# First channel layer of the third batch's first 512 tokens by seven half-width products instead of eight

## The chip, the cores and the metric

One core of one Trainium2 chip. The metric is the device time of one execution in microseconds (us); the times of before are three such executions. TensorE is PE, its weight load PEld, VectorE is DVE, ScalarE is ACT, GpSimd is POOL, and SyncE, which issues every DMA here, is SP.

## The reference

Four batches, 8 heads, 768 tokens of 64 values per head, so 512 values per token. Per batch: attention over a local window and over block means, then a mixer along the tokens and one along the channels.

```python
x  = attention(q, k, v)                  # window |i-j| < 16, and means of blocks of 32
h  = relu(x.T @ w_tok1) @ w_tok2         # 768 -> 256 -> 768 along the tokens
u  = x + h.T
h2 = relu(u @ w_ch1) @ w_ch2             # 512 -> 1536 -> 512 along the channels
out = u + h2
```

All of it is float32.

## The kernel before, in words

**Precision.** A float32 operand is split into a high and a low part, and each product is made of three (high by high, high by low, low by high). So a 128-row weight block against a stretch of tokens costs three matmuls.

**Tiling.** Batches 0 to 2 run through the channel mixer in two parts of 512 and 256 tokens, each in 12 slots, one for a chunk f of 128 of the 1536 channels. In a slot `ch1` (L1018, matmuls at L1027, PSUM tile `hp`) makes the chunk: four weight blocks c=0..3 by three products, 12 matmuls of 512 or 256 columns. ACT writes relu(hp) as the high part of `h` (L1039), DVE the low part (L1044), and `ch2` (L1054, matmuls at L1070, tiles `acc`) adds the chunk's share to the four outputs, again 12 matmuls. `ch1` of a slot stands ahead of `ch2` of the slot before, so PE has work while `h` is split.

**Beside it.** The attention of batch b+1 runs in the slots of batch b: scores `sc` (L513), the scan on DVE that adds the mask and finds each row's lowest (L527, called the mask scan here), exponentials on ACT (L537), a transpose on DVE (L598), the way through DRAM (`away` L602, `eT` L620), and the product with the values `av` (L645). Heads go in pairs: `sc_24` and `sc_25` are the first half of a pair's scores, and pair 12 is the first of batch 3. Near the end of batch b stand `tok1_all` of batch b+1 (tiles `t1q`, L883) and its `tok2` (L942, tiles `up`, L966): DVE adds `up` to the transposed `x` (`xT`, L982), ACT and DVE split the sum into `u` (L990, L996). In batch 2 `tok2` of the 256 tokens stood in slots 2 to 5.

**The last batch** already goes by seven products for eight, with weights that are mixed beforehand: `mixes` (L1127) builds on POOL and ACT four combinations of the weight blocks of a pair of chunks (i, i+6), and SP parks them in DRAM (`mix_w1h`, `mix_w1l` for the first channel layer, L1198). The table `MIXES` says in which slot of which batch each is built.

**What sets the order.** Every piece of work is an entry with an engine, a modelled duration, what it reads and writes, and a rank. A planner (L162) runs through them in modelled time; on each engine the ready entry of the lowest rank goes next. The result is a fixed queue per engine, and an instruction that waits holds all behind it on its engine. SP's queue is one too, and each DMA also waits for the eighth DMA before it.

```python
R_H, R_EVAC, R_ATT, R_LATER, R_W = range(5)
BANKS = {"start": ["att", "att", "acc0", "acc1"], 0: ["att"], 1: ["att", "att", "acc2", "acc3"]}
```

PSUM has two banks for `hp` ("mm"), two for the attention ("att"), and one for each of acc0 to acc3.

Of the kernel before, what the change touches and what calls it, by code (L numbers as in the profile page):

```python
# [10 lines left out]
F32 = mybir.dt.float32  # L11
# [234 lines left out]
def tile_attention_mixer(  # L246
# [72 lines left out]
    state = {"phase": "start", "gate": []}  # L319
# [472 lines left out]
    def tok1(b, p):  # L792
        x2, a = x_t[b, p]
        pt = bank(f"t1p_{b}_{p}", ["mm", "mm", "acc3"])

        def products():
# [16 lines left out]
    def tok1x(b, g):  # L813

        x2 = x2_t[b, g]
# [49 lines left out]
    def tok1_all(b):  # L865

        pts = [att_bank(f"t1q_{b}_{k}") for k in range(DTOK // P)]
        xk = [key for p in range(NP) for key in x_keys(b, p)]
# [71 lines left out]
    T2_KEYS = [(w, (i, k)) for w in (wt2h, wt2l) for i in range(3) for k in range(2)]  # L940

    def tok2(b, half, p):  # L942
        if b == B - 1:
            return tok2_last(half, p)
        (x2, a), t1 = x_t[b, p], t1_t[b, p]
        h0, nt = H0[b][half], HT[b][half]
        pt = bank(
            f"up_{b}_{half}_{p}",
            ["mm", "mm", "acc3"] if state["phase"] == "start" else BANKS[state["phase"]],
# [6 lines left out]
        def products():  # L956
# [17 lines left out]
            reads=([] if far else x_keys(b, p)) + t1_keys(b, p) + T2_KEYS,  # L974
# [41 lines left out]
    h_t = {}  # L1016
# [37 lines left out]
    def ch2(b, half, f):  # L1054
        h, nt = h_t.pop(f), HT[b][half]
        n = 512 // nt
        if f == 0:
# [5 lines left out]
        last = f == NF - 1  # L1063
        slots = [sums[o][0] for o in range(0, NC4, n)]

        def products(os):
            for o in os:
                slot, c0 = sums[o]
                for w, part in (("w2h", 0), ("w2l", 0), ("w2h", 1)):
# [3 lines left out]
                        start=(f == 0 and w == "w2h" and part == 0 and o % n == 0),  # L1073
# [3 lines left out]
        reads = [(h, 0), (h, 1)] + weight_keys(("w2h", "w2l"), f)  # L1077
# [127 lines left out]
    def mixed(name, i, sets, view, keys, behind=()):  # L1205
# [8 lines left out]
            reads=[(src, 0), (src, 1)], writes=keys, kb=131 * (hi - lo), behind=behind,  # L1214
        )

    def mixed_weight(name, i, sets, f, halves, behind=()):
# [3 lines left out]
            weight_keys((name,), f, halves), behind,  # L1221
# [29 lines left out]
    def tok2_last(half, p):  # L1251
        b, t1, u = B - 1, t1_t[B - 1, p], sums_at(half, p)
        pt = bank(f"up_{b}_{half}_{p}", EIGHT if half else BANKS[1])

        def products():
# [10 lines left out]
            "pe", 1.08, products, reads=t1_keys(b, p) + T2_KEYS, writes=[(pt, 0)], rank=R_ATT  # L1266
# [42 lines left out]
    def out_of(pt, to, other, func=AF.Copy):  # L1309
# [15 lines left out]
        )  # L1325

# [616 lines left out]
```

## Time and profile before

| what | value |
|---|---|
| three executions | 558.75, 559.75, 560.01 us; median 559.75 |
| the profiled execution | 557.6 us, its span 555.8 us (1.8 us lie around the span) |
| granted TensorE clock | 1.000 over the span: the 2.4 GHz level |
| PE busy | 543.1 us, 98% of the span |
| DVE, ACT, POOL busy | 330.6, 251.8, 246.7 us (59%, 45%, 44%) |
| DMA | 101.10 MB, mean 182 GB/s |

The page is read as follows: PE is busy nearly all the time, so a change shows in the time either through the time that PE's own instructions take, or through a wait that it brings into PE's queue. The profiled execution is 2.15 us below the median of the three.

### The profile page before, as it was taken

To read this page: it belongs to the slowest core of one execution; us is meant where nothing else is said; L and a number is where in the kernel's file an instruction comes from. 1 tells how busy PE (TensorE), PEld (TensorE's weight loads), DVE (VectorE), ACT (ScalarE), POOL (GpSimd) and SP (SyncE) were. 2 spreads that over 40 slices of the span, in tenths; PEclk is the share of its full clock that TensorE was granted. 3 is DMA by queue.
4 is the path that set the end of the run, shared out by engine and by line. 5 is a ranking of instruction groups with operands and counts; after the bars stand their busy time and mean duration, and the time that the engine had idled before them with its cause. 6 is when DMAs were issued, how large, how long until landed. Compare 5 with 4: busy or idle time off the path is not lost.

```text
span 555.8 us, 12577 instructions
## 1 busy us (share of the span) xinstructions
PE 543.1 (98%) x4549; PEld 478.7 (86%) x4549; DVE 330.6 (59%) x922; ACT 251.8 (45%) x784; POOL 246.7 (44%) x362
## 2 busy tenths in 40 slices
PE   7799999999999999999999999999999999999997
PEld 4589788889989878888799987878889999999997
DVE  5897799988463355553553257344352066569992
ACT  5895666526485443322414325243433443356410
POOL 0356688726383933310058404467869853000000
PEclk9999999999999999999999999999999999999999
DMA  8992568745658147867676216787696543932732
GB/s 294 343 255 85 184 197 261 245 131 190 228 163 256 38 153 208 224 190 210 160 229 157 96 30 202 164 235 199 168 276 147 135 166 116 317 102 86 238 113 86
DMA packets 125743, 101.10 MB, mean 182 GB/s; under 512 B 70000, under 2 KB 105456, under 8 KB 125680
## 3 DMA queue, kind: packets, MB, share of 16 engines
q1 hardware_dynamic: 125680, 100.29, 60.8%
q8 instruction: 36, 0.59, 0.5%
q14 instruction: 27, 0.22, 0.1%
HBM read 70.18 MB, written 28.31 MB: 177 GB/s over the span
## 4 chain that ended last, share of the span: by engine, by line
PE 88%; DVE 5%; POOL 3%; ACT 2%; issue 1%; POOLq 0%; DVEq 0%; ACTq 0%
PE acc L1070 28%; PE hp L1027 27%; PE sc L513 4%; PE av L645 4%; PE t1q L883 3%; PE up L966 3%; PE x L1297 2%; PE y L1297 2%; PE z L1297 2%; PE pz L1297 2%; PE up L1259 2%; PE pw L1297 1%; PE pv L1297 1%; PE px L1297 1%; PE pr L1297 1%; PE w L1297 1%
## 5 line engine op out<-in xcount | busy, mean ns | idle before, releaser
L1070 PE MATMUL acc<-h,w2h 128*128 128x256 f32 (+1 forms) x576 | 153.9, 339 | 0.0
L1027 PE MATMUL hp<-u,w1h 128*128 128x256 f32 (+1 forms) x576 | 143.9, 339 | 0.3 <-DVE u L1010 0.3
L1070 PEld LDWEIGHTS acc<-h,w2h 128*128 128x128 f32 x576 | 100.5, 188 | 13.9 <-ACT h L1039 1.7
L1027 PEld LDWEIGHTS hp<-u,w1h 128*128 128x128 f32 x576 | 98.0, 189 | 12.9 <-issue 1.1
L1027 PE MATMUL hp<-u,w1l 128*128 128x256 f32 (+1 forms) x288 | 96.9, 336 | 0.0
L1070 PE MATMUL acc<-h,w2l 128*128 128x256 f32 (+1 forms) x288 | 96.4, 335 | 0.0
L537 ACT ACTIVATE e<-e,den 128x120 f32<-128x120 f32 x192 | 73.5, 385 | 48.8 <-DVE den L527 37.9
L1044 DVE SCALAR_TENSOR_TENSOR h<-hp,h 128x512 fp32r<-128x512 f32 (+1 forms) x72 | 39.8, 552 | 83.9 <-ACT h L1039 83.8
L1039 ACT ACTIVATE h<-hp 128x512 fp32r<-128x512 f32 (+1 forms) x72 | 35.1, 487 | 104.2 <-PE hp L1027 104.0
L1027 PEld LDWEIGHTS hp<-u,w1l 128*128 128x128 f32 x288 | 54.4, 189 | 5.8
L1070 PEld LDWEIGHTS acc<-h,w2l 128*128 128x128 f32 x288 | 54.2, 188 | 5.2
L527 DVE CUSTOM_DVE_ANT_0 e<-sc,mask_sb 128x120 f32<-128x120 f32 x192 | 41.8, 277 | 14.9 <-PE sc L513 14.3
L537 ACT ACTIVATION_READ_ACCUMULATOR e<-e,den 128x1 f32 x192 | 36.3, 189 | 0.0
L651 POOL TENSOR_SCALAR rec<-den 128x6 f32<-128x6 f32 x32 | 8.5, 266 | 58.7 <-ACT e L537 57.0
L1110 POOL TENSOR_TENSOR ot<-ot,u 128x512 f32<-128x512 f32 (+1 forms) x24 | 24.4, 1045 | 21.4 <-DVE ot L1102 19.9
L469 DVE TENSOR_REDUCE vs<-vb 96x8 f32<-96x256 f32 (+1 forms) x40 | 18.0, 461 | 21.0 <-DMA vb<-in_vb 20.7
L513 PE MATMUL sc<-k,q 64*64 64x120 f32 x768 | 27.7, 271 | 2.2 <-DVE k L390 1.2
L513 PEld LDWEIGHTS sc<-k,q 64*64 64x64 f32 x768 | 20.3, 132 | 10.8 <-issue 7.9
L645 PEld LDWEIGHTS av<-v,eT 120*64 120x64 f32 x768 | 24.1, 138 | 5.3 <-issue 3.5
L966 PE MATMUL up<-wt2h,t 128*128 128x512 f32 (+1 forms) x96 | 28.4, 353 | 0.1
L645 PE MATMUL av<-v,eT 120*64 120x64 f32 x768 | 26.7, 224 | 1.3 <-DVE den L527 0.8
L381 DVE TENSOR_REDUCE ks<-k 128x24 f32<-128x768 f32 x16 | 15.1, 946 | 19.9 <-DMA k<-in_kw 19.8
(248 smaller groups left out, 1042.5 us busy)
## 6 DMA issues: line engine op xcount, KB each, us to landing
w<-in_w_ch SPq DMA_DIRECT2D x48, 256.0 KB
k<-in_kw SPq DMA_DIRECT2D x16, 720.0 KB
v<-in_vw SPq DMA_DIRECT2D x32, 288.0 KB
q<-in_q SPq DMA_DIRECT2D x16, 384.0 KB
away<-e SPq DMA_DIRECT2D x16, 384.0 KB
eT<-away SPq DMA_DIRECT2D x64, 96.0 KB
w<-in_w_tok SPq DMA_DIRECT2D x12, 256.0 KB
vb<-in_vb SPq DMA_DIRECT2D x32, 96.0 KB
```

The costliest lines, as they stand in the source:

```text
L469: lambda: nc.vector.tensor_reduce(out=s.t[:VB, rows], in_=slot.t[:VB], axis=AX, op=ALU.add),
L513: nc.tensor.matmul(tiles[j].t[c * QT : (c + 1) * QT, i * NC : (i + 1) * NC], lhsT=qt.t[rows, t * QT : (t + 1) * QT], rhs=kt.t[rows, t, :], ...
L527: nc.vector.tensor_tensor_reduce(out=e.t[:, j, i * P : i * P + NC], in0=tiles[j].t[:, i * NC : (i + 1) * NC], in1=mask_sb[:, mv, :], op0=A ...
L537: nc.scalar.activation(ei, ei, AF.Exp, bias=den_t[n].t[:, 1, T : T + 1], scale=-1.0, accum_out=den_t[n].t[:, 0, T : T + 1],)
L645: nc.tensor.matmul(pv[cs, T], lhsT=eT[:NC, T % (TT // 2), cs], rhs=v.t[:NC, 2 * T + c], start=True, stop=True,)
L966: nc.tensor.matmul(pt.t[:, :nt], lhsT=t1.t[:, part, ks], rhs=w.t[:, k, h0 : h0 + nt], start=(far and k == 0 and i == 0), stop=(k == DTOK / ...
L1027: nc.tensor.matmul(pt.t[:, :nt], lhsT=block(w, f, c), rhs=us[c].t[:, part], start=(i == 0), stop=(i == len(ops) - 1),)
L1039: lambda: nc.scalar.activation(h.t[:, 0], pt.t[:, :nt], AF.Relu),
L1044: lambda: nc.vector.scalar_tensor_tensor(out=h.t[:, 1], in0=pt.t[:, :nt], scalar=0.0, in1=h.t[:, 0].bitcast(F32), op0=ALU.max, op1=ALU.sub ...
L1070: nc.tensor.matmul(slot.t[:, c0 : c0 + nt], lhsT=block(w, f, o), rhs=h.t[:, part], start=(f == 0 and w == "w2h" and part == 0 and o % n == 0),
L1110: lambda view=view, u=u: nc.gpsimd.tensor_tensor(out=view(), in0=view(), in1=u.t[:, 1].bitcast(F32), op=ALU.add),
L1297: nc.tensor.matmul(pt.t[:, :cols], lhsT=w[wp][0](), rhs=z.t[:, zp], start=first and seen == 0, stop=final and seen == 3 * len(ops) - 1, sk ...
```

## The change

In batch 2 the first channel layer of the first 512 tokens is made in another way for four of the six pairs of chunks, (0,6), (1,7), (2,8) and (5,11). Let the four 128-row blocks of `u` be two halves of the sum and the 512 tokens two halves of 256. A pair is then a 2x2 by 2x2 block product, 8 products of 256 columns, or in the matmuls of before 2 x 12 of 512 columns. It becomes 7 products of 6 matmuls of 256 columns: 42 for 24. The order of the 12 chunks becomes 10, 9, 4, 3, which are made as before, then the pairs.

- **Token side** (`differences`, once, at slot 0 of batch 2): four combinations "1" to "4" of the blocks of `u`, each split again: 8 x (three DVE operations of 128x256 at L1439, an ACT copy at L1447, a low part at L1453 on DVE or POOL). They lie where the token weights lay (tags `wt1`, `wt2h`, `wt2l`), which are therefore parked in DRAM in batch 0 (`keep_token`) and brought back in slots 16 and 18 of batch 2 (`return_token`).
- **Weight side**: the mixed weights of the last batch, 32 loads of 128 KB (`load_set`, L1221) into five half chunks of the plain weights, which are parked and brought back also (`keep_block`, `return_block`, ten DMAs each). The mixes of the second layer move from slots 5 to 9 of batch 2 to batches 0 and 1, others to slots 6 to 12.
- **Per pair**: `first_of` (4 products in the two "mm" banks `s7b`, `s7a`, then one ACT copy and three DVE additions), `second_of` (3 products, two DVE sums, four ACT relus and four DVE low parts of 256 columns, where two and two of 512 stood).
- **Moved for it**: `tok2` of the 256 tokens of batch 2 goes from slots 2 to 5 to slot 0, with `x` in the tag `wt1` (`x_home`) and the banks acc2 and acc3; the attention of batch 3 is spread over another stretch of slots (`A01`).

```diff
-    MIXES = {(0, 12): [('w1', 0, 'h')], ... (2, 5): [('w2', 0, 't1', 0), ('w2', 0, 't1', 1)], ...}
+    MIXES = {
+        ...
+        (0, 8): [("w2", 0, "t1", 0)], (0, 9): [("w2", 0, "t1", 1)],
+        ...
+    }
+    A01 = -4, 25
+    KEEP, BACK = (0, 18, 20, 22), (16, 18, 18)
+    ENDS = [f for f in range(NF) if f % HF not in SEVEN]
+    SEQ = [(0, f) for f in reversed(ENDS)] + [(0, f) for i in SEVEN for f in (i, i + HF)]
...
-            u1s = (2, 3, 4, 5)
+            u1s = (2, 3, 4, 5) if b < SB else (0, 0, 0, 0)
...
+            if b == SB and slot in NEXT:
+                job, i = NEXT[slot]
+                at = job(i)
...
+            if b == SB and slot == 0:
+                differences()
...
+    def differences():
+        ...
+        for to, x, y in (("1", "12", "11"), ("2", "22", "1"), ("3", "22", "12"), ("4", "21", "2")):
+            for c in range(2):
+                ...
+                for (a, i), (d, k), op in (
+                    ((xv, 0), (yv, 0), ALU.subtract), ((None, 0), (xv, 1), ALU.add),
+                    ((None, 0), (yv, 1), ALU.subtract),
+                ):
+                    add("dve", 0.37, ...)
+                add("act", 0.36, ...)
+                eng = "dve" if to in "12" else "pool"
+                add(eng, 0.37 if eng == "dve" else 0.7, ...)
...
+    def first_of(i):
+        B2, A = mm_bank(f"s7b_{i}"), mm_bank(f"s7a_{i}")
+        ...
+            (B2, "w", 0, (ring[i, 0], 0), "2", True, []),
+            (B2, "y", QS, (ring[i, 1], 0), "1", False, [(B2, "w")]),
+            (A, "p", 0, (i, 0), "11", True, []),
+            (A, "x", QS, (ring[i, 2], 0), "3", False, [(A, "p")]),
...
+    def second_of(i):
+            (B2, "y", QS, (ring[i, 3], 0), "22"),
+            (A, "p", 0, (i, 1), "21"),
+            (A, "x", QS, (i + HF, 1), "4"),
```

The planner makes a new order of every engine from this. Three places of it follow. In the names, `up_2_0_3` is batch 2, first part, block 3; `e_12_0` is pair 12, first half.

DVE at the start of batch 2 before the change, from the last `u` on; the first scan of pair 12 stands right behind the splits:

```order
L982 TENSOR_TENSOR xT_2_0_2_4102<-up_2_0_2_4277,xT_2_0_2_4102 128x512
L996 TENSOR_TENSOR u_2_0_1_4296<-xT_2_0_1_4071,u_2_0_1_4296 128x512
L996 TENSOR_TENSOR u_2_0_2_4302<-xT_2_0_2_4102,u_2_0_2_4302 128x512
L982 TENSOR_TENSOR xT_2_0_3_4286<-up_2_0_3_4289,xT_2_0_3_4286 128x512
L996 TENSOR_TENSOR u_2_0_3_4335<-xT_2_0_3_4286,u_2_0_3_4335 128x512
L1044 SCALAR_TENSOR_TENSOR h_1_1_11_4349<-hp_1_1_11_4321,h_1_1_11_4349 128x256
L527 ISA e_12_0_4316,den_24_4391<-sc_24_0_4371,mask_sb_71 128x120
```

The same place of the change. Between `u_2_0_2` and the first mask scan stand the four `x_home` additions and the last output of batch 1 (`ot`):

```order
L1007 TENSOR_TENSOR u_2_0_2_4538<-xT_2_0_2_4358,u_2_0_2_4538 128x512
L993 TENSOR_TENSOR x_home_4370<-up_2_1_0_4530,x_home_4370 128x256
L993 TENSOR_TENSOR x_home_4370<-up_2_1_1_4541,x_home_4370 128x256
L1112 TENSOR_TENSOR ot_1_1_0_4482<-acc_1_1_2_3933,u_1_1_2_3287 128x256
L1112 TENSOR_TENSOR ot_1_1_0_4482<-acc_1_1_2_3933,u_1_1_3_3368 128x256
L993 TENSOR_TENSOR xT_2_0_3_4521<-up_2_0_3_4512,xT_2_0_3_4521 128x512
L993 TENSOR_TENSOR x_home_4370<-up_2_1_2_4561,x_home_4370 128x256
L993 TENSOR_TENSOR x_home_4370<-up_2_1_3_4579,x_home_4370 128x256
L1007 TENSOR_TENSOR u_2_0_3_4603<-xT_2_0_3_4521,u_2_0_3_4603 128x512
L527 ISA e_12_0_4527,den_24_4614<-sc_24_0_4589,mask_sb_71 128x120
```

And between the scans of the two halves of pair 12 in the change stand five operations of the differences, one low part, the transpose and the split of `h`:

```order
L1453 TENSOR_TENSOR diff_wt2h_4607<-diff_tmp_4519,diff_wt2h_4607 128x256
L1439 TENSOR_TENSOR diff_tmp_4519<-diff_tmp_4519,u_2_0_1_4510 128x256 x2
L1439 TENSOR_TENSOR diff_more_4650<-u_2_0_2_4538,diff_wt2h_4607 128x256
L1439 TENSOR_TENSOR diff_more_4650<-diff_more_4650,u_2_0_2_4538 128x256
L1439 TENSOR_TENSOR diff_more_4650<-diff_more_4650,diff_wt2h_4607 128x256
L598 STREAM_TRANSPOSE e_12_0_4527<-e_12_0_4527 128x768
L1055 SCALAR_TENSOR_TENSOR h_2_0_10_4673<-hp_2_0_10_4616,h_2_0_10_4673 128x512
L527 ISA e_12_1_4570,den_24_4614<-sc_24_1_4655,mask_sb_71 128x120
```

So the scans of pair 12 stand behind more work on DVE, and the scores of pair 13 (`sc_26`, `sc_27`) use the banks that they free.

SP before the change, around the four DMAs that bring back pair 13's second half (`eT_13_1`):

```order
L602 DMA away_13_1_4818<-e_13_1_4704 128x768
L1198 DMA mix_w1h_4_4700<-wa_w1_4_1_4737 512x1x128
L1198 DMA mix_w1l_4_4708<-wc_w1_4_1_4814 512x1x128
L620 DMA eT_13_1_4885<-away_13_1_4818 32x24x32 x4
L602 DMA away_14_0_4929<-e_14_0_4887 128x768
```

And in the change. The five loads ahead of it overwrite weight sets which PE must have read; the last of them waits for the second product of `s7b_2`:

```order
L1221 DMA w1h_2_1332<-mix_w1h_5_4210 128x256
L1221 DMA w1l_2_1339<-mix_w1l_5_4250 128x256
L1221 DMA w1h_3_1496<-mix_w1h_5_4210 128x256
L1221 DMA w1l_3_1519<-mix_w1l_5_4250 128x256
L1221 DMA w1h_3_1496<-mix_w1h_5_4210 128x256
L620 DMA eT_13_1_5229<-away_13_1_5125 32x24x32 x4
L1221 DMA w1l_3_1519<-mix_w1l_5_4250 128x256
```

`eT_13_1` now stands behind set loads that are released by PE.

## Rows read from the trace of the kernel before

**Rows 1.** The page: busy time of the engines, and the chain of work that ended last, by engine.

```profile
PE 543.1 (98%) x4549; PEld 478.7 (86%) x4549; DVE 330.6 (59%) x922; ACT 251.8 (45%) x784; POOL 246.7 (44%) x362
PE 88%; DVE 5%; POOL 3%; ACT 2%; issue 1%; POOLq 0%; DVEq 0%; ACTq 0%
```

**Rows 2.** Windows of 25 us: busy time of PE, PEld, DVE, ACT and POOL, the granted clock, the DMA share and GB/s. Batch 2's first part runs from 328.87 to about 409 us.

```profile
225.00:250.00 25.00, 25.00 (x199) 20.23 (x198) 13.61 (x45) 8.66 (x32) 5.39 (x12) 1.00 0.79 217
...
325.00:350.00 25.00, 25.00 (x194) 20.79 (x193) 14.24 (x55) 10.26 (x42) 5.74 (x11) 1.00 0.48 132
350.00:375.00 25.00, 25.00 (x199) 20.38 (x198) 11.02 (x39) 9.02 (x32) 15.58 (x31) 1.00 0.79 209
375.00:400.00 25.00, 25.00 (x191) 20.04 (x190) 9.38 (x35) 9.43 (x36) 20.20 (x40) 1.00 0.80 204
```

**Rows 3.** What PE waited for over the whole span: total us, times, the longest.

```profile
PE et L575 <- DVE x L656: 1.4, 2, 1.1
PE sc L513 <- DVE k L390: 1.2, 1, 1.2
...
PE t1q L846 <- POOL ws L832: 0.7, 1, 0.7
```

**Rows 4.** The chain of work that ended last, in batch 2's first part: start, us, what. Each piece runs to the start of the next.

```profile
341.20 2.75 PE hp L1027 x12
...
347.67 2.72 PE hp L1027 x12
350.39 0.71 PE up L966 x6
351.10 2.75 PE acc L1070 x12
353.84 1.55 PE av L645 x48
355.39 2.94 PE hp L1027 x12
...
380.86 1.55 PE av L645 x48
```

**Rows 5.** The same chain where batch 1 ends and batch 2 begins. The last `t1q` of batch 2 ends at 316.16.

```profile
314.80 1.36 PE t1q L883 x6
316.16 1.42 PE acc L1070 x12
317.57 1.44 PE hp L1027 x12
319.02 5.60 PE up L966 x24
324.62 1.41 PE acc L1070 x12
326.03 1.43 PE hp L1027 x12
327.46 1.42 PE acc L1070 x12
328.87 2.76 PE hp L1027 x12
331.63 0.78 PE sc L513 x24
```

**Rows 6.** DVE there: start, us, operation, shapes, count, and the idle time before it.

```profile
316.51 2.20 DVE L907 SCALAR_TENSOR_TENSOR t<-t1q,t 128x128 fp32r<-128x128 f32 x7 [0.39 <-ACT t L900]
...
320.46 0.69 DVE L982 TENSOR_TENSOR xT<-up,xT 128x512 f32<-128x512 f32 x1 [0.50 <-PE up L966]
321.90 0.69 DVE L996 TENSOR_TENSOR u<-xT,u 128x512 fp32r<-128x512 f32 x1 [0.75 <-ACT u L990]
...
333.35 1.46 DVE L1102 TENSOR_TENSOR ot<-acc,u 128x256 f32<-128x256 f32 x4
...
336.62 0.98 DVE L598 STREAM_TRANSPOSE e<-e 128x768 f32<-128x768 f32 x1 [0.81 <-ACT e L537]
337.59 0.28 DVE L527 CUSTOM_DVE_ANT_0 e<-sc,mask_sb 128x120 f32<-128x120 f32 x1
337.80 0.08 DVE L527 DVE_READ_ACCUMULATOR2_ANT den<- 128x1 f32 x1
337.80 0.28 DVE L527 CUSTOM_DVE_ANT_0 e<-sc,mask_sb 128x120 f32<-128x120 f32 x1
```

**Rows 7.** ACT there: exponentials of one half of a pair, six in all, and the first of the split of `h`.

```profile
338.37 0.38 ACT L537 ACTIVATE e<-e,den 128x120 f32<-128x120 f32 x1
...
338.75 0.38 ACT L537 ACTIVATE e<-e,den 128x120 f32<-128x120 f32 x1
...
339.51 0.57 ACT L1039 ACTIVATE h<-hp 128x512 fp32r<-128x512 f32 x1
```

**Rows 8.** SP's issues in batch 2: start, us, what. The four `eT` of 372.33 are pair 13's second half, whose `av` began at 380.86 by the chain.

```profile
372.33 2.75 SPq L620 DMA_DIRECT2D eT<-away  x4
...
381.75 0.35 SPq L338 DMA_DIRECT2D v<-in_vw  x1
```

**Rows 9.** PE where batch 1's first token layer waits for POOL.

```profile
189.94 1.34 PE L846 MATMUL t1q<-xs,ws 128*128 128x256 f32 x9 [0.69 <-POOL ws L832]
```

**Rows 10.** The weight loads between 325 and 409 us: count, busy us, mean ns, idle.

```profile
L1027 PEld LDWEIGHTS hp<-u,w1h 128*128 128x128 f32 x105 | 18.9, 188 | 3.7 <-issue 0.2
```

More of the change, by code (lines that the diff above doesn't have):

```diff
@@ L1052, in tile_attention_mixer, with ch2 @@
     acc = {}
-    def ch2(b, half, f):
+    def ch2(b, half, f, first, last):
         h, nt = h_t.pop(f), HT[b][half]
         n = 512 // nt
-        if f == 0:
+        if first:
             for o in range(NC4):
@@ L1203, in mixes, with mixed @@
             )
-    def mixed(name, i, sets, view, keys, behind=()):
+    def mixed(name, i, sets, view, keys, behind=(), kb=131):
         src = mix_t[name, i]
@@ L1325, in out_of, with keep_block @@
         )
+    SB, QS, R_D = B - 2, HT[0][0] // 2, R_ATT
+    SEVEN = (0, 1, 2, 5)
+    kept, T_t = {}, {}
+    def keep_block(f, behind=()):
+        for n in ("w1h", "w1l"):
+            to = kept[n, f] = plan.slot(dram, [P, 256], F32, f"kept_{n}_{f}", f"kept_{n}_{f}", 1)
+            add(
+                "sp", 0.06,
+                lambda n=n, to=to: nc.sync.dma_start(
+                    out=to.t, in_=weight(n, f)[:, :256].bitcast(F32)
+                ),
+                reads=weight_keys((n,), f, (0,)), writes=[(to, 0)], kb=96, behind=behind,
+            )
@@ new lines, in return_block, with keep_token @@
+    def return_block(f, behind=()):
+        for n in ("w1h", "w1l"):
+            src = kept[n, f]
+            add(
+                "sp", 0.06,
+                lambda n=n, src=src: nc.sync.dma_start(
+                    out=weight(n, f)[:, :256].bitcast(F32), in_=src.t
+                ),
+                reads=[(src, 0)], writes=weight_keys((n,), f, (0,)), kb=96, behind=behind,
+            )
+    def keep_token(n, behind=()):
+        w = state["wt1"] if n == 2 else state["wt2"][n]
+        cols = TT * DTOK
+        to = kept[n] = plan.slot(dram, [P, cols], F32, f"kept_t{n}", f"kept_t{n}", 1)
+        keys = [(w, i) for i in range(3)] if n == 2 else [
+            (w, (i, k)) for i in range(3) for k in range(2)
+        ]
+        add(
+            "sp", 0.06,
+            lambda: nc.sync.dma_start(out=to.t, in_=in_rows(w.t, n)),
+            reads=keys, writes=[(to, 0)], kb=580, behind=behind,
+        )
@@ new lines, in in_rows, with return_token @@
+    def in_rows(t, n):
+        return (t if n == 2 else t.bitcast(F32)).rearrange("p a c -> p (a c)")
+    def return_token(n, behind=()):
+        src = kept[n]
+        shape, dtype, tag = (
+            ([P, TT, DTOK], F32, "wt1") if n == 2
+            else ([P, DTOK // P, S], F32R, ("wt2h", "wt2l")[n])
+        )
+        w = plan.slot(const, shape, dtype, tag, f"{tag}_again", 1)
+        if n == 2:
+            state["wt1"] = w
+            keys = [(w, i) for i in range(3)]
+        else:
+            state["wt2"] = tuple(w if i == n else x for i, x in enumerate(state["wt2"]))
+            keys = [(w, (i, k)) for i in range(3) for k in range(2)]
+        add(
+            "sp", 0.06,
+            lambda: nc.sync.dma_start(out=in_rows(w.t, n), in_=src.t),
+            reads=[(src, 0)], writes=keys, kb=580, behind=behind,
+        )
@@ new lines, in tile_attention_mixer, with load_set, part_product, run @@
+    RING = [f for f in range(HF, NF) if f != HF + 4]
+    ring, seven = {}, {}
+    def load_set(j, k):
+        n = 4 * j + k
+        f, i = RING[n % len(RING)], SEVEN[j]
+        ring[i, k] = f
+        s = (2, 1, 0, 3)[k]
+        for name in ("w1h", "w1l"):
+            mixed_weight(name, i, (s, s + 1), f, (0,), kb=96)
+    def part_product(ws, zs, slot, key, c0, start, final, behind_key=None):
+        def run():
+            seen = 0
+            for w, z in zip(ws, zs):
+                for wp, zp in ((0, 0), (0, 1), (1, 0)):
+                    nc.tensor.matmul(
+                        slot.t[:, c0 : c0 + QS], lhsT=w[wp](), rhs=z.t[:, zp],
+                        start=start and seen == 0, stop=final and seen == 5,
+                        skip_group_check=True,
+                    )
+                    seen += 1
+        return run
```

220 lines of the change are left out of this document (197 added, 23 removed), and 13 rows, old and new, of the table MIXES.

## The prediction

> **What bounds the kernel now.** The page first: PE is busy for 98% of the span and has 88% of the chain that ended last [rows 1]. That alone doesn't say that PE bounds every stage, so the windows come next: in batch 2's first part, which the change rewrites, PE is busy 25.00 of 25 us in each window, at granted clock 1.00, while DVE is at 9.4 to 14.2 and POOL at 5.7 to 20.2 [rows 2]. The reader is to see two things there: nothing but PE's own work takes time in that stage, and the other engines have room, but not much of it on one place is promised by an average. The waits of PE agree: the largest sum over the whole span is 1.4 us, and the largest entries belong to other stages [rows 3]. So the time falls by what PE's queue gets shorter, and rises by any wait that enters it. The chain with its start times gives the price of each piece of PE's work [rows 4], and the rows where batch 1 ends give the work of PE and DVE at the place where the change puts most of its additions [rows 5, 6].
>
> **What PE saves.** Twelve matmuls of 512 columns take 2.72 us, start to start [rows 4], so 227 ns each; twelve of 256 take 1.43 [rows 5], so 119 ns. A pair takes 24 x 227 = 5.45 us before and 42 x 119 = 5.00 to 5.04 after (3.5 groups of 1.43 to 1.44). That is 0.41 us for a pair and **1.65 us for four**, 0.3%: halved columns cost 0.525 of whole ones, so of the eighth that the arithmetic saves (0.68 us for a pair) three fifths are left. Bounds: 1.6 and 1.75.
>
> Weight loads are what could spoil this, since 42 stand where 24 stood. A load is recorded with 188 ns in this stretch [rows 10], more than the 119 ns from one 256-column matmul to the next; so the loads overlap each other or the matmuls, and the 119 ns hold with a load for every matmul. The Trainium skill (TensorE: Matmul & The Clock Gate, Back-to-back issue gap) says that in a stream of load and matmul the spacing is set by both, and that the formula by columns alone counts too little for few columns. The trace agrees only in part: spacing is above half, 119 for 113.5, and not at the load's own duration.
>
> **What the start of batch 2 costs.** Here is the disputed term. I take T0 as the end of the last `t1q`, and follow both engines in the order that the change gives them.
>
> PE, without waits: a group of `acc` 1.42, half of one 0.71, four `up` of 512 columns 5.60 [rows 5]; two `up` of 256 at 0.71 [rows 4], half a group 0.71, two more `up` 1.42, scores 0.78 [rows 5], first `hp` of batch 2 2.75, scores 0.78, second `hp` 2.94 [rows 4]. So PE comes to the scores of pair 13 (`sc_26`) at T0 + 18.5.
>
> DVE: the low parts of `t1` and the first two `ot` are done by T0 + 3.7 (2.20 for seven, 1.46 for four [rows 6]). `up_2_0_1` ends at 2.13 + 2.8 = 4.9. From there stand three `xT` and four `u` of 512 at 0.69, and four `x_home`, two `ot` and four differences of 256 at 0.365 [rows 6]: 4.83 + 3.65 = 8.5. The first mask scan of pair 12 thus begins at T0 + 13.4 and its six take 1.25 (pitch 0.20 [rows 6]): 14.7. Then six operations of the differences 2.2, the transpose 0.98, the split of `h` 0.69 and six scans 1.25, together 5.1: **19.8**. The exponentials, six at 0.38 [rows 7], end at about 16.5 and hold nothing. `sc_26` and `sc_27` need the two banks that these last scans free, so PE waits 19.8 - 18.5 = **1.3 us**; smaller waits before (the second pair of `x_home`, and `sc_25` behind the last `xT`, 0.4 each) lie inside it, since DVE's chain is the same. In the rows of before the four `u` are followed by the scans at once, and 4.25 us of PE's work (324.62 to 328.87) cover the last of them [rows 5, 6]. Bounds: 0 if DVE is 1.3 us quicker than I add up; 2.6 if each of some fifteen hand-overs between engines costs another 0.1 us. I take 1.35.
>
> **What the rest costs.** *Differences and the pairs' evacuation on DVE*: 28 operations for the differences, and for each pair nine of 256 columns where two of 512 stood, 3.3 for 1.4 us: 10.2 + 7.6 = 18 us in a stretch of 50 in which DVE has 14.24 + 11.02 [rows 2], so 43 of 50. Between the last product in a bank and the next pair's first product in it stand at least 2.2 us of PE's work (two groups of six and a score group), and DVE needs a sum of 0.37 and whatever stands ahead of it, at most a transpose. I take 0.2; bounds 0 and 2.5.
>
> *Set loads on SP*: a load waits until PE has read what it overwrites, and holds the queue. The load just ahead of `eT_13_1` is released at the end of the second product of `s7b_2`; from there to `av_26` PE has 1.44 + 2.72 + 0.71 + 0.71 = 5.6 us. A load's issue takes 0.35 and the four `eT` 2.75 [rows 8], so 2.5 us are left to land; before there were 5.8, from 375.08 to 380.86 [rows 4, 8]. I take 0.3; bounds 0 and 3.3 (landing as long as the cover of before).
>
> *Traffic*: 32 loads of 128 KB, 4.2 MB, come into the stretch whose DMA share is 0.48 to 0.80 [rows 2], but the mixes that leave it wrote about as much. In batch 1 the share is 0.79 around 225 to 250 us [rows 2], where two mixes arrive; nothing on PE's path there is late. Parking the token weights and blocks has slots of time. Nothing for these, bounds 0 and 0.5.
>
> *Batch 0*: the mixes that arrive on POOL stand at the lowest rank and fill idle time. The one wait of PE for POOL, 0.69 us before a `t1q` [rows 9], now has one more group of `acc` ahead of it and may shrink: I take -0.2, bounds -0.7 and 0. *The last batch* keeps its own work; all eight `up` of it stand together, as the chain of before has them nearly: nothing.
>
> **Sum**: -1.65 + 1.35 + 0.2 + 0.3 - 0.2 = 0.0 against the profiled 557.6 us, which lies 2.15 below the median of the three; so **559.8 us** for a median like that of before. A measurement of this kernel tells about 0.2%, 1.1 us, from no change.
>
> **The rivals.**
>
> *DVE's queue holds, the saving stays.* If DVE ends the scans before PE comes to `sc_26`, only the small terms are left: -1.65 + 0.1 - 0.2, so 558.0. For it: every PE price above is measured, PE has no wait in this stage now [rows 2, 3], and my 1.3 us is the difference of two sums of 20 us. Against it: DVE's sum holds only durations of the trace, and no hand-over. 0.30.
>
> *SP's queue makes `av_26` late.* Slower. It decides at a landing of over 2.5 us for `eT_13_1`; each us beyond is one on PE, and with the 1.35 of the start the time is 561.2 at a landing of 4 and 563 at the bound. For it: the load ahead can't be issued before PE's own products, and the DMA share there is 0.80 [rows 2]. Against it: the cover is 5.6 us of PE's work. 0.15.
>
> *DVE becomes the bound through the pairs.* 43 of 50 us busy leaves 7, and in-order work that waits for PE and ACT by turns may not fit: 0.6 us a pair comes to +2.4, so 562.2. It decides at a queue of more than 1.8 us ahead of a pair's last sum. 0.12.
>
> *The weight load sets the spacing.* [...] As a mechanism here: 42 x 188 - 24 x 227 = 2.45 us for a pair, +9.8 in all, 569. The 1.43 us for twelve [rows 5] speak against it. 0.01.
>
> **How the numbers follow.** My forecast, the saving eaten at the start of batch 2, has 0.42, with its own range 558.7 to 560.9. The faster rival has 0.30, the slower ones 0.28. The range that leaves out 2 in 10 runs from 557.8, a little under the faster case, to 562.2, the third rival's value; it takes in the bound of 2.6 at the start and the lower half of SP's.
>
> **What would show it.** Right: twelve products of 256 at 1.43 in the new code, no wait inside the pairs, and in PE's waits 1 to 2 us in scores or `up` for DVE between the last `t1q` of batch 2 and its third `hp`. Wrong: no such wait and about 1.7 us less, or a wait of `av` for the `eT` DMAs, or of `s7a`/`s7b` for DVE's sums. A spacing of the new products above 125 ns would upset the first term.

## The result: 0.7% slower, outside the forecast range

| what | before | the change |
|---|---|---|
| median of the runs timed side by side | 558.5 us (557.61 to 561.34, 10 runs) | 562.46 us (561.06 to 566.13, 10 runs) |
| ratio, 95% interval | | 1.0070 [1.0041, 1.0099] |
| profiled execution, its span | 557.6, 555.8 us | 562.02, 560.2 us |

A second measurement gave 1.0077 [1.0052, 1.0102]. The forecast was no change, 559.8 us, with a range up to 562.2; slower by over 0.2% had a chance of 0.28.

### The profile after

The page's busy line answers to [rows 1], and its first line to read is PE's share: PE's busy time is 0.5 us longer and the span 4.4, so most of the difference is time in which PE was idle; the busy time also holds matmuls that ran at the lower clock, which hide what the products saved. The transfers grew by 11.55 MB (101.10 before).

```profile
PE 543.6 (97%) x4621; PEld 484.4 (86%) x4621; DVE 352.7 (63%) x978; ACT 257.7 (46%) x806; POOL 253.0 (45%) x374
DMA packets 135920, 112.65 MB, mean 201 GB/s; under 512 B 70960, under 2 KB 115120, under 8 KB 135856
```

PE's waits over the span (total us, times, the longest), to be held against [rows 3]. "z <- sums_t" is new, and "sc <- issue" stands at 2.6 where before had one of 0.7 in its first 20 us; the entry for `k` belongs to the first microseconds of the kernel, which differ from run to run (see the repeated profile of before, below).

```profile
PE sc L513 <- DVE k L390: 2.8, 2, 2.0
PE sc L513 <- issue: 2.6, 1, 2.6
...
PE z L1308 <- ACT sums_t L1325: 0.8, 1, 0.8
```

Where the 2.6 stands is told by the chain (start, us, what) at the same place as [rows 5]. The last `t1q` of batch 2 ends at 321.47, the T0 of the prediction.

```profile
331.61 0.42 DVE x_home L993
332.03 0.04 issue
332.08 1.68 PE up L977 x12
333.76 0.78 PE sc L513 x24
334.53 2.95 PE hp L1038 x12
337.48 0.78 PE sc L513 x24
338.26 2.96 PE hp L1038 x12
341.22 2.63 issue
343.86 1.09 PE sc L513 x24
344.94 4.53 PE acc L1080 x12
```

The reader is to see three things. The order is the one that the prediction walked: scores, `hp`, scores, `hp`, and then a hole of 2.63 us ahead of `sc_26`. A second `x_home` pair also had PE waiting (0.83 us by the starts of the matmuls). And behind the hole the scores take 1.09 for 0.78 and a group of `acc` 4.53 for 2.95. The windows (PE, PEld, DVE, ACT, POOL, granted clock, DMA share, GB/s) say why: the clock is granted at 1.00 up to the end of the hole and stands at the lower level, 1.2 GHz (0.50), from 346 to 348 us.

```profile
340.00:342.00 2.00, 1.21 (x6) 0.67 (x4) 1.97 (x3) 0.69 (x2) 1.51 (x3) 1.00 0.93 358
342.00:344.00 2.00, 0.14 (x2) 0.17 (x2) 2.00 (x15) 0.99 (x6) 1.81 (x4) 1.00 0.86 316
344.00:346.00 2.00, 2.00 (x27) 1.59 (x27) 1.97 (x5) 2.00 (x10) 0.45 (x3) 0.81 0.58 150
346.00:348.00 2.00, 2.00 (x6) 1.57 (x5) 2.00 (x4) 1.24 (x4) 1.92 (x4) 0.50 0.28 78
348.00:350.00 2.00, 2.00 (x8) 1.56 (x8) 1.90 (x6) 0.00 (x0) 0.51 (x1) 0.84 0.92 286
325.00:350.00 25.00, 21.68 (x160) 17.33 (x159) 23.79 (x63) 12.51 (x42) 16.91 (x28) 0.93 0.47 145
```

The last of these is the window of [rows 2]: DVE went from 14.24 to 23.79 us of 25, POOL from 5.74 to 16.91. What DVE did ahead of the hole (start, us, operation, shapes, count) shows more than its busy share. Compare the 128x256 additions with the 0.365 us of [rows 6], and the 128x512 `u` with the 0.69 there:

```profile
330.46 1.23 DVE L1007 TENSOR_TENSOR u<-xT,u 128x512 fp32r<-128x512 f32 x1
331.61 0.74 DVE L993 TENSOR_TENSOR x_home<-up,x_home 128x256 f32<-128x256 f32 x2
...
336.58 0.87 DVE L1453 TENSOR_TENSOR diff_wt2h<-diff_tmp,diff_wt2h 128x256 fp32r<-128x256 f32 x1
337.37 1.55 DVE L1439 TENSOR_TENSOR diff_tmp<-diff_tmp,u 128x256 f32<-128x256 f32 x2
338.84 0.68 DVE L1439 TENSOR_TENSOR diff_more<-u,diff_wt2h 128x256 f32<-128x256 f32 x1
339.55 0.85 DVE L1439 TENSOR_TENSOR diff_more<-diff_more,u 128x256 f32<-128x256 f32 x1
340.44 0.84 DVE L1439 TENSOR_TENSOR diff_more<-diff_more,diff_wt2h 128x256 f32<-128x256 f32 x1
```

POOL at the same time. L1151 and L1173 belong to a mix of weights for the last batch (`w1`, pair 4) that the table places in slot 4 of batch 2; at the lowest rank it was ready at once and filled POOL's first idle time, which is here. Between its operations POOL also makes low parts of `u` and an `ot`:

```profile
330.13 2.15 POOL L1151 TENSOR_TENSOR wa_w<-w1h,w1l 128x256 f32<-128x256 f32 x2 [1.11 <-DMA xT<-xaway]
...
337.99 0.64 POOL L1173 TENSOR_TENSOR wc_w<-wc_w,wa_w 128x128 f32<-128x128 f32 x1
338.71 0.52 POOL L1173 TENSOR_TENSOR wc_w<-wa_w,wc_w 128x128 f32<-128x128 f32 x1
339.20 1.80 POOL L1151 TENSOR_TENSOR wa_w<-w1h,w1l 128x256 f32<-128x256 f32 x2
```

While POOL is busy, a DVE operation that reads two SBUF operands takes 1.8 to 2.4 times as long (0.68 to 0.87 for 0.365, and 1.23 for 0.69); `x_home`, one of whose operands is in PSUM, keeps 0.74 for two. Six operations of the differences take 4.62 us (336.58 to 341.20) where the prediction has 2.2.

The pairs themselves run as forecast:

```profile
360.38 1.43 PE s7b L1477 x12
361.81 1.44 PE s7a L1477 x12
```

### Where the time went

PE's time is split here, stretch by stretch, into a usual pitch for each kind of matmul and what lies above it, worked out from the starts of all matmuls. Before is taken from a second profile of it (span 557.0), since its first one had a kernel start 1.7 us quicker by the third pair's `av` (34.25 against 35.98 us; the change 35.65). The clock tells the two apart: from 10 to 20 us it was granted at 1.00 in the first profile, and at 0.66 in the second and in the change. The split by stretch is rough: with one median pitch for each shape of matmul, batch 1 comes to -0.8 and the rest of batch 2 to +0.2, while the start of batch 2 stays at +5.3.

| stretch | change less before, us |
|---|---|
| matmuls at their usual pitch | -1.96 |
| batch 0, to 200 us | -0.64 |
| batch 1, 200 to 300 us | -1.14 |
| end of batch 1 and start of batch 2, 300 to 360 us | +5.30 |
| pairs and the rest of batch 2, 360 to 460 us | +0.70 |
| last batch | +1.15 |
| sum | +3.41 |

The +5.30 is read off nearly whole: waits of 0.83 and 2.81 us (by the matmuls' starts), and at the lower clock 0.31 on the scores and 1.58 on the group of `acc`. The last batch's 1.15 is mostly one wait of 0.98 us at `z` for `sums_t`, and it looks like the same cause a second time. The chain there leads from `z` back through ACT and DVE to two `zx` operations on two SBUF operands, which took 2.28 us beside POOL:

```profile
468.79 2.28 DVE L1255 TENSOR_TENSOR zx<-ut,zx 128x384 fp32r<-128x384 f32 x2
...
469.32 1.33 POOL L1255 TENSOR_TENSOR z<-uf,z 128x384 fp32r<-128x384 f32 x1
```

In the run `quiet` (below), where `z` doesn't wait, one takes 0.56:

```profile
472.54 0.56 DVE L1255 TENSOR_TENSOR zx<-ut,zx 128x384 fp32r<-128x384 f32 x1 [0.59 <-ACT zx L1250]
```

PE's order differs too: between the eight `up` and `z` stand 0.72 us of `acc` in the change and 2.83 in `quiet` and `plain`. No run parts POOL from the order here, so this is not shown.

### The profile page after: what moved, and what is told of

Its sections match the earlier page's. It is cut to its first block, busy times and chain, and to the rows that moved or that the text cites. A ratio compares the mean times of both kernels' runs of the same rounds, so it can differ in the third digit from the quotient of the medians.

```text
span 560.2 us, 12888 instructions
## 1 busy us (share of the span) xinstructions
PE 543.6 (97%) x4621; PEld 484.4 (86%) x4621; DVE 352.7 (63%) x978; ACT 257.7 (46%) x806; POOL 253.0 (45%) x374
## 4 chain that ended last, share of the span: by engine, by line
PE 85%; DVE 5%; DMA 3%; POOL 2%; issue 2%; SPq 2%; ACT 1%; DVEq 0%; POOLq 0%; ACTq 0%
PE acc L1080 27%; PE hp L1038 23%; PE sc L513 4%; PE av L645 3%; PE x L1308 2%; PE y L1308 2%; PE pz L1308 2%; PE t1q L891 2%; PE s7a L1477 2%; PE up L977 2%; PE s7b L1477 2%; PE t1q L853 2%; PE z L1308 2%; PE up L1270 2%; DMA k<-in_kw 1%
## 5 line engine op out<-in xcount | busy, mean ns | idle before, releaser
L1038 PE MATMUL hp<-u,w1h 128*128 128x256 f32 (+1 forms) x512 | 124.2, 333 | 0.3 <-DVE u L1021 0.3
L1038 PEld LDWEIGHTS hp<-u,w1h 128*128 128x128 f32 x512 | 86.3, 189 | 10.9 <-issue 1.3
L1038 PE MATMUL hp<-u,w1l 128*128 128x256 f32 (+1 forms) x256 | 84.4, 330 | 0.0
L1055 DVE SCALAR_TENSOR_TENSOR h<-hp,h 128x256 fp32r<-128x256 f32 (+1 forms) x64 | 34.3, 536 | 78.7 <-ACT h L1050 78.5
L1050 ACT ACTIVATE h<-hp 128x256 fp32r<-128x256 f32 (+1 forms) x64 | 30.4, 474 | 84.0 <-PE hp L1038 83.8
L1038 PEld LDWEIGHTS hp<-u,w1l 128*128 128x128 f32 x256 | 48.4, 189 | 4.5
L496 POOL MEMSET e<- 128x48 f32 x16 | 2.2, 138 | 53.2 <-DMA away<-e 29.1
```

What stands on the lines that cost most here:

```text
L1038: nc.tensor.matmul(pt.t[:, :nt], lhsT=block(w, f, c), rhs=us[c].t[:, part], start=(i == 0), stop=(i == len(ops) - 1),)
L1050: lambda: nc.scalar.activation(h.t[:, 0], pt.t[:, :nt], AF.Relu),
L1055: lambda: nc.vector.scalar_tensor_tensor(out=h.t[:, 1], in0=pt.t[:, :nt], scalar=0.0, in1=h.t[:, 0].bitcast(F32), op0=ALU.max, op1=ALU.sub ...
```

## The experiments

The theory after the result: DVE's queue at the start of batch 2 is the cause, as forecast, and it is longer than added up because POOL's mix stretches DVE's operations. Rivals: the wait has another cause (a load on SP, the exponentials), or the pairs cost more than they save.

### The suspected cost by itself

`micro` leaves out the kernel's computation: sixteen or twelve additions on DVE, first without POOL, then beside twenty additions of 128x256 on POOL, with both DVE operands in SBUF or one in PSUM. The 512 columns have no time alone in it, since POOL's twenty additions from the part before still ran beside them.

```diff
+    for x, w, n in ((a, 256, 16), (pa, 256, 16), (a, 512, 12)):   # a in SBUF, pa in PSUM
+        dve(n, x, w, ...)          # alone
+        pool(20, [], [])
+        dve(n, x, w, [], [])       # beside POOL
```

> None of the kernel's computation: DVE additions of 128x256 alone and then beside twenty POOL additions of 128x256, all of POOL's operands in SBUF. Three kinds: both operands of DVE in SBUF; one in PSUM; both in SBUF with 512 columns. Theory A (the two engines take turns for operands from SBUF): alone 0.35, 0.36, 0.62 us from one to the next; beside POOL the first kind 0.6-0.8 and the third 0.8-1.1, the second unchanged. Theory B (the longer differences come from hand-overs and DMA): no kind changes by more than 10%.

DVE's timeline, `ma` in SBUF and `mp` in PSUM:

```profile
2.98 5.43 DVE L286 TENSOR_TENSOR mr<-ma,mb 128x256 f32<-128x256 f32 x16
...
9.48 13.36 DVE L286 TENSOR_TENSOR mr<-ma,mb 128x256 f32<-128x256 f32 x16
22.77 5.38 DVE L286 TENSOR_TENSOR mr<-mp,mb 128x256 f32<-128x256 f32 x16
...
29.06 5.38 DVE L286 TENSOR_TENSOR mr<-mp,mb 128x256 f32<-128x256 f32 x16
```

And POOL's beside the second and the fourth of them:

```profile
9.53 16.64 POOL L298 TENSOR_TENSOR mg<-mc,md 128x256 f32<-128x256 f32 x20 [0.54 <-DVE ma L321]
...
29.22 19.06 POOL L298 TENSOR_TENSOR mg<-mc,md 128x256 f32<-128x256 f32 x20 [0.54 <-DVE ma L321]
```

An addition of two SBUF operands goes from 5.43 / 16 = 0.34 us to 13.36 / 16 = 0.83 beside POOL; with one operand in PSUM it stays at 0.34. POOL's take 16.64 / 20 = 0.83 there, so the two engines take the same 0.83 per operation. The Trainium skill (SBUF — State Buffer, Who interferes with whom) says that a DVE instruction with two SBUF inputs contends with a GpSimd instruction that reads SBUF, and that one with at most one SBUF input, outside DVE's two-port modes, does not. The trace agrees with both (0.83 and 0.34 for 0.34 alone). The two don't simply take turns, though: one of each, one after the other, would be 0.34 + 0.72 (POOL's single addition) = 1.06 us, and 0.83 was measured, so a part of each does overlap.

### Filling the hole, quieting POOL, plain products

Four kernels in one series (before 557.43). `after_again` is the change once more.

> The change unedited, as the base of this call. Theory A (two operands from SBUF: DVE's subtractions and splits are stretched while POOL builds a mix, the mask scans come late, PE waits and its clock falls) and theory B (the DVE queue is too long even at its own durations) both expect about 562, PE waits of 0.7 and 2.6 us at the start of batch 2, acc at half clock behind the second.

562.63 (559.4 to 563.35), 1.0077 [1.0052, 1.0102]: waits of 0.83 and 2.83 at the same places, and the clock lower behind them again (0.89 from 335 to 350 us).

`fill` computes the chunk 9 of batch 2 twice, so PE has 12 products more ahead of `sc_26`:

```diff
+            for again in range(2 if (b, half, f) == (SB, 0, 9) else 1):
```

> The unedited change with the second chunk of batch 2 (f=9) computed twice into the same bank, 12 matmuls more, 2.72 us of work just ahead of the place where PE waits. If the fall of the clock comes from the wait, the wait goes to about 0, the clock stays at 1.00, and the time falls by the 1.9 us that the slow stretch costs (sc 1.09 for 0.78, acc 4.53 for 2.95), to about 560; if the clock falls for another reason, the time rises by the 2.7 us less the wait, that is 0 to 0.5.

561.69 (560.42 to 562.28), 1.0065 [1.0046, 1.0084]. The wait is gone and the clock stays at 1.00, so about 2.7 us more work on PE came out no slower than the change. The hole was therefore idle time that PE could fill, and the slow clock went with it. The time stays above the 560 expected; one `av` waits 0.95 us for its `eT`, and `z` waits as in the change.

`quiet` holds the mixes of batch 2 until their own slot, so POOL's mix no longer runs at the start. DVE's order there is the same.

```diff
-                mixes(*job, behind=here if slot > 14 else ())
+                mixes(*job, behind=here if slot > 14 or b == SB else ())
```

> The change with POOL's mixes of batch 2 released one by one with their slot, so that the mix of pair 4 no longer runs at the start of the batch; DVE's order there is the same. Theory A: the six operations between the two halves' scans go from 4.6 us to 2.3-2.8, the wait at the scores of pair 13 from 2.65 to 0.2-1.0, granted clock 1.00 there, and the time falls by 2.5 to 4 us against the unedited change, to 558-559.5. Theory B: the wait stays at 2 us or more and the time within 1 us of the unedited change.

560.97 (559.42 to 562.15), 1.0054 [1.0036, 1.0072]. DVE at the differences, as above:

```profile
336.28 1.42 DVE L1439 TENSOR_TENSOR diff_tmp<-diff_tmp,u 128x256 f32<-128x256 f32 x2
337.61 0.42 DVE L1439 TENSOR_TENSOR diff_more<-u,diff_wt2h 128x256 f32<-128x256 f32 x1
338.06 0.42 DVE L1439 TENSOR_TENSOR diff_more<-diff_more,u 128x256 f32<-128x256 f32 x1
338.52 0.42 DVE L1439 TENSOR_TENSOR diff_more<-diff_more,diff_wt2h 128x256 f32<-128x256 f32 x1
```

Only the pair of `diff_tmp`, which still begins beside POOL's low parts of `u` (to 336.95), is stretched; the `diff_wt2h` ahead of it, beside POOL too, took 0.44, so not every operation there is. The waits fall from 0.83 and 2.83 to 0.29 and 1.00, and the clock stays at 1.00 there. This is the decisive run: with POOL quiet the term measures 1.29 us, where the prediction had 1.35. But only 1.7 us of about 5.2 (2.4 of waits, 1.9 of clock, and the wait of `z`, which is gone too) came back, less than the 2.5 to 4 expected, and the intervals of the two runs overlap. The pairs now wait, and behind their waits the clock falls again (0.50 from 384 to 386 us). PE's waits:

```profile
PE s7b L1477 <- DVE diff_more L1578: 1.9, 1, 1.9
...
PE s7a L1477 <- DVE diff_tmp L1520: 0.9, 1, 0.9
```

The chain there (start, us, what) leads through DVE to two transfers:

```profile
364.36 7.05 DMA k<-in_kw
...
372.48 4.33 DMA away<-e
...
376.84 0.05 DVE e L527
...
378.33 0.99 PE s7a L1477 x6
```

A mask scan of the attention waited for `away` to leave the tile it writes, and the sums of the pair stood behind it in DVE's queue. The DMA share is 1.05 from 365 to 376 us, where [rows 2] have 0.79 and 0.80.

`plain` keeps the new order, the differences and the mixes, but makes all 12 chunks as before and loads no sets.

```diff
-    SEVEN = (0, 1, 2, 5)
+    SEVEN = ()
```

> All parts of the change but the seven products: the pairs' chunks are made by 12 matmuls of 512 columns as before, without loads of mixed weights; the differences are still built, parking and moves stay. If the products save what the first term of the sum says, this is 1.65 us slower than the unedited change, at the same waits at the start of batch 2: 563-564.5. If the pairs' evacuation or the set loads cost PE what the products save, it is equal to the unedited change within 0.5.

560.99 (559.92 to 562.13), 1.0059 [1.0037, 1.0081]. The waits at the start are the same (0.83, 2.83), so neither SP's loads nor the pairs make them. The clock did not fall behind them this time, and `z` did not wait. So with 1.65 us more of product work it came out 1.6 us quicker than the change, not 1.65 slower as expected; the intervals overlap, so the 1.6 isn't sure. The 1.9 of clock and 1.0 at `z` are more than the pairs give. No run therefore shows the saving in the time itself, only in PE's own pitch.

### Taking the work away from the start

`early` moves the mixes of batch 2's start to slots 10 and 11 of batch 1, and the others to slots 12 and 21 of batch 2:

```diff
-        (2, 4): [("w1", 4, "t1", 0)],
-        (2, 6): [("w1", 4, "t1", 1)],
+        (1, 10): [("w1", 4, "t1", 0)],
+        (1, 11): [("w1", 4, "t1", 1)],
+        (2, 21): [("w2", 4, "h")],
...
```

> The change with the mixes of pair 4 of the first layer moved to slots 10 and 11 of batch 1 and those of the second layer's pairs 5 and 4 to slots 12 and 21 of batch 2, so that the first part of batch 2 has no mix at all: POOL quiet, and 3 MB less traffic beside the 32 loads of mixed weights. Theory A with the traffic as second part: wait at the scores of pair 13 1.0 us as in the run before, no wait of s7a or s7b, clock 1.00: 1.5 to 2.5 us less than that run, 558.5-559.5, within 0.4% of the kernel before. Theory B (the pairs themselves are too much for DVE): s7a and s7b still wait for over 1 us and the time stays at 560.5-561.5.

569.07 (567.65 to 569.44), 1.0202 [1.0189, 1.0215]: a miss. No wait of `sc_26` is listed, but the `up` behind `x_home` waits 1.2 us by the matmuls' starts, so the start of batch 2 costs about what it cost in `quiet`. A `s7a` waits 1.2 us, an `av` 1.7, and near the end of batch 2 `acc` waits 3.9 for ACT's `h`, which stood behind a split of the returned token weights. The clock falls behind both places (0.79 from 380 to 388 us, 0.50 from 444 to 450). The chain at the second:

```profile
438.41 4.96 DMA wt_again<-kept_t
...
443.40 0.02 ACT ws L927
```

`late_diff` is `early` with the differences held until slot 1, so they leave the space between the scans:

```diff
-            if b == SB and slot == 0:
-                differences()
+            if b == SB and slot == 1:
+                differences(here)          # behind=here on the three additions
```

> The same as the last one, and the differences released a slot later, so that both halves of pair 12's scans stand ahead of them on DVE. If the differences in DVE's queue are what makes the scans late, the wait at the scores of pair 13 goes from 1.0 to 0-0.3 and the time falls by 0.7-1.0 more, unless the first product of the first pair (s7b) then waits for the differences; 557.5-558.5, equal to the kernel before or up to 0.2% under it.

561.02 (557.55 to 563.3), 1.0063 [1.0039, 1.0088]; its times lie in two groups, near 558 to 560 and 562 to 563, and what parts them isn't settled. In the profile (559.32 us) both the wait of `sc_26` and the slow clock are gone (0.78 is left at `x_home`), and the last wait has moved to the pairs: 2.8 us of `s7a` for DVE, which waited for a transfer (chain: `v<-vs`, 4.25 us from 385.14, DMA share 0.91 from 380 to 392).

`late_only` is the change with the differences late, the mixes left where the change has them:

> The change with nothing but the differences released a slot later; mixes as in the change. If the place of the differences in DVE's queue alone makes the wait at the scores of pair 13, it goes from 2.65 to 0-0.3 with POOL's mix still beside them, the clock stays at 1.00 there, and the time falls by 3 us or more, unless the time comes back in the pairs (theory C: the set loads and the attention's DMAs share SP and the DMA engines, and the pairs wait for DVE, which waits for a DMA): then waits of s7a or s7b of 1-3 us and 560-561.5.

563.74 (561.14 to 564.91), 1.0099 [1.0077, 1.0122]. Both waits at the start are gone with POOL's mix still there, so they need the differences between the scans; without the mix (`quiet`) 1.29 us of them stay, so the mix sets their size. The time is over the 561.5 expected: `s7a` waits 2.6 for DVE, with the clock at 0.74 behind it (360 to 365 us), and `t1q` 2.4 for POOL.

`late_plain` is `late_diff` with plain products and no set loads:

> The run with late differences and early mixes, its pairs made by 12 matmuls of 512 columns and no loads of mixed weights. Theory C: without the 32 loads no wait of 1 us or more is left after the start of batch 2; what remains over the kernel before are the waits of the second pair of up for x_home, 0.8 us: 558.0-558.6. If the waits in the pairs' stretch come from DVE's or POOL's work and not from the loads, they stay, with 560 or more.

562.22 (561.54 to 564.83), 1.0083 [1.0061, 1.0106], against 558.0 to 558.6 expected. No wait is left in the stretch of the pairs, so those of `late_diff` come from the loads and the pairs' own DVE work, between which this run doesn't part. Near the end of batch 2 `acc` waits 2.0 for ACT's `h`, and `t1q` 1.3 for POOL, whose mix waited for transfers behind the return of the token weights, which landed after 7.6 us.

`before_again` is a second profile of the kernel before:

> The kernel before, a second profile. All profiles of the changed kernel spend 0.9 to 2.0 us more in their first 40 us than the one profile of before, where the two do the same work. If that belongs to the change, this profile has its first av of the third pair at 34.2 us again; if it varies from run to run, it lies anywhere in 34.2-35.8.

558.73 us. Its start is like the change's, the lower clock there included, and one `av` waits 0.67 us for its DMA at 270 us.

### Fewer pairs, an earlier return

`late_two` is `late_diff` with two pairs, 16 loads, of which fewer come at once (two sets in slot 0 and three in slot 3, for five in slot 0):

```diff
-    SEVEN = (0, 1, 2, 5)
+    SEVEN = (0, 1)
```

> The run with late differences and early mixes, with two pairs, (0,6) and (1,7), by seven products, and so 16 loads for 32. Half of the saving, 0.8-1.0 us. Theory C: half the loads leave the attention's DMAs room, no wait of 1 us or more in the pairs, and the time is 557.0-557.8, equal to the kernel before or just under it. Otherwise a wait in the pairs stays and the time is above 558.5.

562.13 (561.28 to 567.27), 1.0091 [1.0058, 1.0124], against 557.0 to 557.8 expected. No wait of 1 us in the pairs, but `acc` waits 2.9 at 436 us for the returned weights (landing 5.72 us).

`two_back` brings the token weights back in slots 13 and 15, and holds POOL's and ACT's splits of them until slot 20:

```diff
-    KEEP, BACK = (0, 18, 20, 22), (16, 18, 18)
+    KEEP, BACK = (0, 18, 20, 22), (13, 15, 15)
```

> The run with two pairs, and the token weights brought back in slots 13 and 15 for 16 and 18, their use held to slot 20. Theory: what cost 3 us there at 436 was the return of the token weights, 768 KB that landed 5.7 us after its issue while ACT's queue stood behind it. Then this wait is gone and the time is 562.1 - 3.0 = 558-559.3, or less if the late runs of that kernel came from it. If the wait of acc for ACT stays, the mix beside it is the cause and the time stays above 561.

557.83 (556.73 to 562.7), 1.0013 [0.9994, 1.0032]: level with before. Left are 0.81 at `up` and 0.95 + 0.41 at `t1q` for POOL.

`three_back` has a third pair:

> As two_back with three pairs: 24 loads, three quarters of the saving. Theory C (the loads crowd the attention's DMAs): a wait in the pairs between that of two pairs (none) and of four (3.1 us): 0-1.5, and 557.5-559.5.

558.27 (556.76 to 560.16), 1.0014 [0.9999, 1.0028], with no wait of `s7a` or `s7b`.

`four_back` has all four:

> As two_back with all four pairs, so the run with late differences and early mixes, with the earlier return. The wait in the pairs (3.1 us in one profile, and times from 557.5 to 563.3) stays if it comes from the set loads: 559-562; the wait of acc or t1q behind the return is absent.

567.16 (562.91 to 568.58), 1.0161 [1.0131, 1.0191]. `s7a` waits 2.3, with the clock at 0.50 behind it (394 to 396 us), `av` 1.1, and `t1q` 3.6 for POOL, which was expected to be absent. So with 32 loads the waits in the pairs come back, with 24 they don't; the fourth pair brings its own DVE work as well, so this doesn't part the loads from it.

`two_best` and `three_best` move the mix that holds `t1q` up, from slot 21 of batch 2 to slot 14 of batch 1:

```diff
-        (2, 21): [("w2", 4, "h")],
+        (1, 14): [("w2", 4, "h")],
```

> two_back with one edit: the last of the three late mixes of weight rows, w2_4, moves on POOL from slot 21 of batch 2 to slot 14 of batch 1. Theory (each removed wait gives its time back unless the cover is gone): the waits of t1q for POOL's xs in batch 2 of two_back (0.95 + 0.41 us) go, since POOL has no mix left there, and the time is 556.5 to 557.3 us, 0.1 to 0.2% under the kernel before. Rival (the wait moves): the mix now stands among POOL's splits for batch 2, t1q of batch 2 waits for POOL about as long, and the time stays at 557.5 to 558.5 us.

> three_back with the same edit (w2_4's mix on POOL from slot 21 of batch 2 to slot 14 of batch 1). Theory: the waits of t1q for POOL's xs (0.90 + 0.65 us in three_back) go, and with a third pair of chunks, worth 0.4 us more than two pairs, the time is 556.5 to 557.5 us. Rival: the wait moves to t1q of batch 2 or to av for eT, and the time stays at 558 to 559 us.

561.02 (560.17 to 563.87), 1.0071 [1.0047, 1.0095], and 559.66 (558.18 to 560.92), 1.0039 [1.0023, 1.0054]: `two_best` is slower than without the edit; the interval of `three_best` overlaps that of `three_back`. For `two_best` the rival holds, and further than it said. PE's waits in `two_best`:

```profile
PE up L977 <- DVE x_home L993: 1.7, 1, 1.7
...
PE z L1308 <- ACT sums_t L1325: 0.8, 1, 0.8
PE t1q L891 <- POOL xs L935: 0.7, 1, 0.7
```

In `two_best` POOL's mix stands among its splits for batch 2 (so `t1q` waits), and the planner's new order puts four additions `ot` on DVE, which stood at 319.56 in `two_back`, at 331.58 (1.41 us) ahead of `x_home`: the `up` behind it waits 1.9 by the matmuls' starts, for 0.81. No version tried has a median below that of the kernel before.

## Why the prediction was wrong, point by point

- **What PE saves: right in PE's own work.** Twelve products of 256 columns at 1.43 to 1.44, so 120 ns each with a load for each, and -1.96 us at the usual pitch for all of PE's matmuls. The rival of the weight load's spacing is out.
- **What the start of batch 2 costs: the step that failed.** Place, order and cause were as written: DVE's second scans free the banks of `sc_26`. The size was not: 3.64 us of waits against 1.35 and a bound of 2.6. The scans ended at T0 + 22.5, not 19.8; PE came at T0 + 19.75, its own sum 18.5, 0.83 of the wait at `x_home` and some 0.4 more. DVE's excess is the differences' (4.62 for 2.2) and two `u` (1.23 and 1.12 for 0.69). The durations of [rows 6] couldn't show it: the 0.69 came from a place where POOL stood idle, and the 0.365 from `ot`, one of whose operands is `acc` in PSUM. The prediction has no word on POOL at the start of batch 2; of its mixes it says only, for batch 0, that they fill idle time. `quiet` and `micro` show what was missing: without POOL's mix the term is 1.29.
- **A consequence that wasn't priced.** The hole was followed by a stretch at the lower clock, 1.9 us more. A bound for a wait has to add it. It followed in both profiles of the change, and not behind the same wait in `plain`. It also followed waits of 1.7 to 3.9 in `quiet`, `early`, `late_only` and `four_back`, and not those of 2.8 in `late_diff` and 2.9 in `late_two`; why isn't settled.
- **The pairs' evacuation: no wait in the change** (0.2 taken). But this was luck of the order: with the start mended, 0.9 to 2.8 us came up there in `quiet` and `late_diff`. The rival "DVE becomes the bound through the pairs" has the right place; its mechanism was a wait for a transfer inside DVE's queue, not DVE's busy time.
- **Set loads on SP, `av_26` late: no such wait in the change.** In the variants the DMA share rises to 1.05 and the attention's transfers land after 4 to 7 us; with 24 loads or fewer no `s7a` or `s7b` waited as much as 0.5 us. So the loads are a likely price once the start is mended, though no run parts them from the pairs' DVE work.
- **Traffic at nothing: true of the change's first profile, not of its second**, where an `av` waits 1.2 us for its `eT` at 438 us, **nor of the variants**, where the token weights returned late (landing 5 to 8 us; waits of 2.0 to 3.9 at `acc`).
- **Batch 0: -0.2 taken**, about -0.6 by the table, of which 0.3 is the kernel's start (35.98 less 35.65); the repeated profile of before doesn't have the 0.69 us wait of [rows 9] either, so it wasn't the change's.
- **The last batch at nothing: wrong by 1.0.** `z` waited 0.98 for `sums_t`. The wait stands in the four profiles (the change twice, `fill`, `two_best`) in which two `zx` took 2.28 us beside POOL and only 0.72 of `acc` covered them, and not in `plain` or `quiet`, where a `zx` took 0.56. In `early` and `late_two` two `zx` took 2.13 with as little cover, and PE waited only 0.48, at `w`. So the same mispriced operations are the likely cause, together with PE's order; no run was made for it.

The sum with what was measured: -1.65 + 3.64 + 1.9 + 1.0 = 4.9 us, of which batches 0 and 1 gave back some by the table; the medians of the two differ by 4.0.

## What to carry to other kernels

Before you price added VectorE work, look at what GpSimd does in the same microseconds, after the change as well as before it: operations with two SBUF operands took 2.5 times as long beside it in `micro` and 1.8 to 2.4 times in the kernel, those with one in PSUM did not. Where a planner may pull filler work of another engine forward, its price is where it lands and not where the table puts it. When 1.65 us are to be gained, each removed wait uncovers the next (DVE, then transfers, then the returned weights); here it took four edits (the mixes earlier, the differences later, fewer pairs, an earlier return) to come back to the time of before.

## What the runs showed that was not expected

- DVE and POOL, both on 128x256 additions from SBUF, took 0.83 us per operation each (alone 0.34 on DVE, 0.72 on POOL for a single one).
- POOL's additions took 19.06 / 20 = 0.95 us in the stretch that begins beside DVE's PSUM form and goes on beside its 128x512 SBUF form, which took 13.22 / 12 = 1.10 us each; the stretch isn't parted further.
- The same wait of 2.8 us at the same place was followed by the lower clock in both profiles of the change (0.50 from 346 to 348 us in the first, 0.59 in the second) and by 1.00 throughout in `plain`. In `late_diff` a wait of 2.8 inside the pairs also left it at 1.00, while in `quiet` waits of 0.9 and 1.9 there were followed by 0.50.
- The kernel before itself differs so from run to run: from 10 to 20 us its clock was 1.00 in one profile and 0.66 in the other, and the second was 1.7 us later by 36 us.
- At a DMA share of 0.9 to 1.05 single transfers of the attention took 4 to 7 us from issue to landing (`away` 4.33, `v` 4.25, `k` 7.05).
